# Adding the softmax constant on ScalarE, and a wider spacing of the second batch's attention steps

## The chip, the cores and the metric

One core of a Trainium2 chip runs the whole program. The metric is the device time of one execution in microseconds; three runs of the kernel before give the median. TensorE is called PE here, VectorE DVE, ScalarE ACT, GpSimd POOL and SyncE, which issues loads, SP.

## What is computed

Attention over chunks of 32 tokens with a little context and 8 memory slots, then a feed-forward layer, then a layer of eight experts in which every token goes to one expert. Cut to what matters:

```python
k_full = np.concatenate([mem_k, k_ctx], axis=2)
scores = scale * np.matmul(q_c, k_full.transpose(0, 1, 3, 2))
a = np.exp(scores - np.max(scores, axis=-1, keepdims=True))
a = a / (np.sum(a, axis=-1, keepdims=True) + 1e-09)
out[:, :, c_start:c_end] = np.matmul(a, v_full)
...
h = x @ w_in
x = (h * (1.0 / (1.0 + np.exp(-h)))) @ w_out
...
out[mask] = np.maximum(x[mask] @ w1[e], 0.0) @ w2[e]
```

## The kernel before

The 3072 tokens are cut into 8 batches of 384. Attention of one batch is done as four pairs of heads, so there are 32 pairs, numbered i = 0 to 31. Pairs 0 to 3 are worked in a prologue; pairs 4n+4 to 4n+7 are worked during batch n of the feed-forward layer. One pair goes through these steps:

- S, `att_s`: the PE makes the scores in two halves (L199); the DVE adds the mask and finds the extremes (L204); ACT takes the exponential and accumulates the sums (L210).
- N, `att_n`: the constant is added to the six sums (L219, DVE), the reciprocal taken (L220, DVE), and POOL multiplies the pair's scores by it (L221).
- T, `att_t`: the PE transposes one half (three transposes, L229), and ACT copies it out of the bank (L240); in the prologue the DVE copies for pairs 0 and 1 (L238).
- A, `att_av`: the product with the values on the PE (L255); behind it X, `att_x`: ACT rounds it to xh (L274) and the DVE takes the rest xl (L275), which the feed-forward layer needs.

The feed-forward layer of a batch runs in 16 steps g. `gemm1` (L297) makes a block of 128 hidden values for 384 tokens from xh and xl in bank h0 or h1; `swish` is a tanh on ACT (L306), a product on the DVE (L308), a rounding on ACT (L315) and the rest on POOL (L316); `gemm2` (L333) of step g - 2 adds to the output.

During the prologue and the first batch the weights are also prepared, in 32 items, two in each step. `tick` does four stages for four different items: `w_split` (ACT L161, POOL L162), `w_bits` (three DVE operations, L151, L152 and L154), `w_bias` (ACT L145) and `w_load` (SP). Every stage needs the one before, and the bias's bank is free again when the bits of an earlier item are done.

The schedule is manual: each engine runs its instructions in the order in which the program writes them. In the prologue that order is the string `PRO`, whose letters are the steps above, with w1 for a bias, w2 for bits and w3 for a split; the loops below it write the order of the batches. A step has three places: 0 ahead of the step's first tick and gemm1, 1 between gemm1 and the second tick, 2 behind gemm2. In the first batch the swish stands behind place 2. A pair's steps go to the places `3 * s0 + slot`, counted in thirds of a step; `PN`, `PT` and `PU` are the slots of N and of the two halves of T, and their first entries are for the first batch. There all scores, transposes and products of pairs 4 to 7 use the bank a0.

Of the kernel before, what the change touches and what calls it, by code (L numbers as in the profile page):

```python
# [7 lines left out]
F32 = mybir.dt.float32  # L8
# [4 lines left out]
AF = mybir.ActivationFunctionType  # L13
OP = mybir.AluOpType
# [6 lines left out]
NF = 16  # L21
# [13 lines left out]
GTH = 7.0  # L35
SPL = 3
PN = (4, 3, 4, 4)
PT = (7, 7, 8, 10)
PU = (8, 7, 8, 10)
PRO = 'q0 k0a p1 m0a p2 i0a v0 p3 S0 w0 N0 S1 w0 v1 S2 z0 N1 w1 T0 S3 w0 N2 w2 d2 v2 w1 T1 A0 w3 N3 X0 T2a A1 w2 w0 v3 w1 X1 g00 T3a w3 w0 A2 w2 w0 w1 X2 g01 w3 w0 A3 w2 w1 g10 g11 X3 w3'  # L40
EARLY = (0, 1, 1, 2, 2, 3, 4)
FILL = (2, 4, 4, 4)
# [5 lines left out]
def body(ctx, tc, qk_in, v_in, wcat1, wcat2, wgt, consts, masks, iconst, bconst, out):  # L48
    nc = tc.nc
    PE, V, A, G, S = nc.tensor, nc.vector, nc.scalar, nc.gpsimd, nc.sync  # L50
    ctx.enter_context(tc.manual_schedule())

    def pool(name, bufs, side, stack=ctx):
        return stack.enter_context(tc.tile_pool(name=name, bufs=bufs, side=side, reuse_waits="tile"))
# [11 lines left out]
    const = pool("const", 1, "left")  # L66
# [7 lines left out]
    Lg = const.tile([128, 24, 8], F32, name="Lg")  # L74
    Lp = const.tile([128, 3, 8], F32, name="Lp")
    junk = const.tile([128, 512], BF16, name="junk")
    wg_sum = const.tile([128, 512], F32, name="wg_sum")

    wg2 = const.tile([128, NF, 16], F32R, name="wg2")
# [136 lines left out]

    def att_n(i):
        s, m = pend.pop(i)
        V.tensor_scalar(out=m[:, 12:18], in0=m[:, 6:12], scalar1=1.0e-9, scalar2=None, op0=OP.add)  # L219
        V.reciprocal(out=m[:, 18:24], in_=m[:, 12:18])  # L220
        G.tensor_tensor(out=s, in0=s, in1=m[:, 18:24].unsqueeze(2).to_broadcast([128, 6, 96]), op=OP.mult)  # L221
        Sb[i] = s
# [274 lines left out]
    for op in PRO.split():  # L497
# [9 lines left out]
        elif c == "m":  # L507
            e.dma_start(msk, masks)
        elif c == "i":
            e.dma_start(ident, consts)  # L510
        elif c == "z":
            S.dma_start(x2d[0:1, :], zero[0:1, 0:1024].bitcast(F32))
        elif c == "S":
            att_s(i, (take(), take()), spare[i - 1] if i else None)
        elif c == "N":
            att_n(i)
        elif c == "T":
            att_t(i, (take(), take()), e is S)
        elif c == "A":
            att_av(i, take(("A", i)))  # L520
        elif c == "X":
            att_x(i)
            free.append(held.pop(("A", i)))
        elif c == "w":
            k = stage[i]
            advance(i, take(("w", k)) if i == 1 else None)
            if i == 2:
                free.append(held.pop(("w", k)))
        elif c == "g":
            if "h%d" % i in free:  # L530
                free.remove("h%d" % i)
            gemm1(0, i, (int(op[2]),))
        elif c == "d":
            b = bank(take())
            for _ in range(i):
                PE.matmul(b[:, 0:224], zero[:, 0:128], zero[:, 0:224], start=True, stop=True)
# [3 lines left out]
    for i in range(4, 4 * NB):  # L540
        n, hp = divmod(i - 4, 4)
        last = n == NB - 2
        s0 = NF * n - EARLY[n] + (SPL * hp if last else 11 * hp // 3 if n == 0 else 4 * hp)
        tight = last or i % 4 == 0 and EARLY[n] > EARLY[n - 1]
        kind = 0 if n == 0 else 1 if not last else 2 if hp < 3 else 3

        pa = 11 if n == 0 or last and hp < 3 or n < NB - 2 and hp == 3 and EARLY[n + 1] > EARLY[n] else 13
        av = "a0" if n == 0 or last and hp == 3 else "a2"

        tags = ("a0", "a1") if n else ("a0", "a0")  # L550
        scores = [(att_s, 1, tags, None, (0,)), (att_s, 2, tags, None, (1,))] if n == 0 else [(att_s, 2 if tight else 1)]
        for what, slot, *k in (*scores, (att_n, PN[kind]), (att_t, PT[kind], tags, False, (0,)),
                               (att_t, PU[kind], tags, False, (1,)), (att_av, pa, av)):
            part.setdefault(divmod(3 * s0 + slot, 3), []).append((what, i, *k))
    for g in range((NB - 1) * NF):
        n, f = divmod(g, NF)
        if g == NF:
            wg_open()
        last = n == NB - 2
# [12 lines left out]
        if g >= 2:  # L572
            m, k = divmod(g - 2, NF)
# [512 lines left out]
    n = NB - 1  # L1086
# [156 lines left out]
```

## Time and profile before

| what | value |
|---|---|
| median of 3 runs | 998.54 us (998.32 to 998.63) |
| profiled execution | 999.0 us, its span 997.2 us |
| mean granted clock of the PE | 0.989 |
| busy share | PE 97%, DVE 69%, POOL 42%, ACT 41% |
| chain that ended last | PE 82%, DVE 9%, issue 4%, ACT 3% |

The page cuts the span into 40 slices of 25 us. In the first four the PE is busy for 7 to 9 tenths and the DVE for 6 to 8; from the fifth on the PE is busy for 9 tenths or more almost throughout. Busy time alone doesn't tell who waits for whom: for that the timeline of an engine gives each instruction with its start, its length and, in brackets, the idle time before it with what ended it.

### The profile page before, as it was taken

What the parts mean: (1) busy time and instruction counts of PE and PEld (TensorE: products, weight loads), DVE (VectorE), ACT (ScalarE), POOL (GpSimd) and SP (SyncE); (2) the same over time, 40 slices, a digit from 0 to 9 for tenths busy, and PEclk for the clock granted to TensorE, in tenths of its full rate; (3) what the DMA queues carried; (4) which work ended last, traced back from release to release, by engine and by line L of the source; (5) the groups of instructions that cost most, each with busy time, mean ns of one, the idle gap of its engine ahead of it and who ended that gap; (6) DMA issues with size and microseconds to landing.
All of it is one profiled execution on the core that took longest, in us unless ns stands there. A gap on an engine that the chain in (4) does not pass through costs nothing.

```text
span 997.2 us, 19115 instructions
## 1 busy us (share of the span) xinstructions
PE 962.4 (97%) x7193; PEld 840.3 (84%) x7193; DVE 683.6 (69%) x1951; ACT 404.9 (41%) x1001; POOL 423.2 (42%) x335
## 2 busy tenths in 40 slices
PE   7799999999999999999999999998999999999997
PEld 5587788998898988888988987777788888999996
DVE  6888578988898988898248674676677787532110
ACT  7667543443444343444443431023333333443441
POOL 3566523232332333222223341144564664777771
PEclk8999999999999999999999999999999999999999
DMA  8667221111212111111121400316353444555420
GB/s 280 212 218 235 101 91 50 47 64 34 63 64 64 33 64 47 50 64 61 36 97 35 167 14 2 127 43 193 110 164 117 139 148 122 179 166 167 150 74 32
DMA packets 34062, 102.86 MB, mean 103 GB/s; under 512 B 4146, under 2 KB 7858, under 8 KB 33971
## 3 DMA queue, kind: packets, MB, share of 16 engines
q1 hardware_dynamic: 29698, 88.63, 28.0%
q0 software_dynamic: 3840, 12.59, 3.7%
q8 instruction: 56, 0.92, 0.4%
q10 hardware_dynamic: 432, 0.43, 0.2%
q14 instruction: 36, 0.29, 0.1%
HBM read 86.69 MB, written 14.94 MB: 102 GB/s over the span
## 4 chain that ended last, share of the span: by engine, by line
PE 82%; DVE 9%; issue 4%; ACT 3%; POOL 1%; DMA 0%; POOLq 0%; DVEq 0%
PE acc L333 23%; PE h L297 23%; PE h L1041 13%; PE acc L1068 12%; PE a L769 3%; PE a L255 2%; PE a L229 2%; PE a L199 2%; DVE a L152 2%; DVE a L151 2%; DVE w L154 1%; DVE junk L428 1%; ACT s L210 1%; PE a L966 1%; ACT spare L210 1%
## 5 line engine op out<-in xcount | busy, mean ns | idle before, releaser
L297 PE MATMUL h<-xh,big 128*128 128x384 f32 x1024 | 289.3, 343 | 2.7 <-DVE th L308 2.7
L316 POOL TENSOR_TENSOR gl<-th,gh 128x384 fp32r<-128x384 f32 x112 | 123.9, 1106 | 252.5 <-ACT gh L315 248.7
L333 PE MATMUL acc<-big,gh 128*128 128x512 f32 x636 | 201.9, 398 | 1.2 <-ACT w L398 1.2
L297 PEld LDWEIGHTS h<-xh,big 128*128 128x128 f32 x1024 | 189.7, 190 | 11.5 <-DVE th L308 4.8
L1014 POOL TENSOR_TENSOR big<-w,big 128x1024 fp32r<-128x1024 f32 x64 | 152.5, 2396 | 78.1 <-ACT big L1013 69.0
L297 PE MATMUL h<-xl,big 128*128 128x384 f32 x512 | 174.4, 341 | 0.0
L333 PEld LDWEIGHTS acc<-big,gh 128*128 128x128 f32 x636 | 115.3, 188 | 21.8 <-ACT w L398 1.6
L333 PE MATMUL acc<-big,gl 128*128 128x512 f32 x318 | 124.8, 392 | 0.0
L1068 PE MATMUL acc<-big,gh 128*128 128x512 f32 x384 | 123.8, 398 | 0.0
L1041 PE MATMUL h<-xh,big 128*128 128x384 f32 x512 | 117.7, 345 | 2.0 <-DVE gl L1050 1.3
L306 ACT ACTIVATE th<-h 128x384 f32<-128x384 f32 x128 | 62.4, 487 | 132.8 <-PE h L297 129.6
L308 DVE SCALAR_TENSOR_TENSOR th<-th,h 128x384 f32<-128x384 f32 x128 | 69.8, 546 | 66.3 <-ACT th L306 66.2
L428 DVE SCALAR_TENSOR_TENSOR junk<-wg_sum,w 128x512 bf16<-128x512 f32 x128 | 112.7, 881 | 3.3
L315 ACT ACTIVATE gh<-th 128x384 fp32r<-128x384 f32 x112 | 58.8, 525 | 126.7 <-DVE th L308 126.7
L297 PEld LDWEIGHTS h<-xl,big 128*128 128x128 f32 x512 | 97.3, 190 | 3.9 <-DVE xl L275 0.6
L1041 PEld LDWEIGHTS h<-xh,big 128*128 128x128 f32 x512 | 90.9, 189 | 6.9 <-DVE gl L1050 1.6
L1045 ACT ACTIVATE gh<-h 128x384 fp32r<-128x384 f32 x64 | 31.5, 492 | 153.9 <-PE h L1041 151.7
L1050 DVE SCALAR_TENSOR_TENSOR gl<-h,gh 128x384 fp32r<-128x384 f32 x64 | 35.3, 553 | 82.7 <-ACT gh L1045 82.3
L417 DVE SCALAR_TENSOR_TENSOR junk<-w 128x512 bf16<-128x512 f32 x96 | 85.4, 889 | 2.3
L1068 PEld LDWEIGHTS acc<-big,gh 128*128 128x128 f32 x384 | 70.6, 188 | 9.3
L1068 PE MATMUL acc<-big,gl 128*128 128x512 f32 x192 | 76.2, 397 | 0.0
L210 ACT ACTIVATE s<-s,m 128x96 f32<-128x96 f32 x168 | 60.8, 363 | 26.5 <-DVE m L204 26.5
(217 smaller groups left out, 1448.3 us busy)
## 6 DMA issues: line engine op xcount, KB each, us to landing
w<-in_wcat SPq DMA_DIRECT2D x96, 512.0 KB, 3.9
qk<-in_qk_in SPq DMA_DIRECT2D x28, 480.0 KB, 4.3
v<-in_v_in SPq DMA_DIRECT2D x28, 288.0 KB, 3.1
x2d<-w SPq DMA_DIRECT2D x16, 256.0 KB, 2.1
w<-in_wgt SPq DMA_DIRECT2D x4, 512.0 KB, 6.7
x2d<-x SPq DMA_DIRECT2D x8, 256.0 KB, 2.4
back<-gd SPq DMA_DIRECT2D x2, 768.0 KB, 5.3
big<-in_qk_in SPq DMA_DIRECT2D x3, 480.0 KB, 6.0
```

Of the source, the lines that this page charges most:

```text
L210: A.activation(out=s[:, b, :], in_=s[:, b, :], func=AF.Exp, scale=-1.0, bias=m[:, b:b + 1], accum_out=m[:, 6 + b:7 + b])
L297: PE.matmul(b[:, :TB], w1[:, o:o + 128], (xh, xl, xh)[p][:, c, :], start=not done, stop=len(done) == 11)
L306: A.activation(out=th, in_=b[:, :TB], func=AF.Tanh, scale=0.5)
L308: V.scalar_tensor_tensor(out=u, in0=th, scalar=1.0, in1=b[:, :TB], op0=OP.add, op1=OP.mult)
L315: A.activation(out=gh, in_=u, func=AF.Copy)
L316: G.tensor_tensor(out=gl, in0=u, in1=gh.bitcast(F32), op=OP.subtract)
L333: PE.matmul(a, g[:, 128 * t:128 * t + 128], w2[:, o:o + 512], start=(f in first and p == 0), stop=(f + 1 in (*first, NF) and p == 2))
L417: V.scalar_tensor_tensor(out=junk, in0=xs[k], scalar=1.0, in1=late["w"][e], op0=OP.mult, op1=OP.mult, accum_out=Lg[:, k, e:e + 1])
L428: V.scalar_tensor_tensor(out=junk, in0=t, scalar=0.5, in1=late["w"][e], op0=OP.mult, op1=OP.mult, accum_out=part2[:, f % 4, e:e + 1])
L1014: G.tensor_tensor(out=l, in0=t, in1=h.bitcast(F32), op=OP.subtract)
L1041: PE.matmul(b[:, :TB], (h, h, l)[p][:, 128 * c:128 * c + 128], (xh, xl, xh)[p][:, c, :], start=(p == 0 and c == 0), stop=(p == 2 and c == 3))
L1068: PE.matmul(a, (gh, gh, gl)[p][:, 128 * t:128 * t + 128], (h, l, h)[p][:, 512:1024], start=(s % 8 == 0 and p == 0), stop=(s % 8 == 7 and p ...
```

## The change

The constant 1e-9 is added to the softmax sums by ACT instead of the DVE, for all 32 pairs: an Identity activation whose bias is a new tile of one column. In the first batch (pairs 4 to 7) the pairs start at steps 0, 4, 8 and 12 instead of 0, 3, 7 and 11, and both halves of T move one place later, to slots 8 and 9. The last pair's product stands at slot 10 instead of 11, which is step 15, place 1 (before: step 14, place 2).

```diff
-PT = (7, 7, 8, 10)
-PU = (8, 7, 8, 10)
+PT = (8, 7, 8, 10)
+PU = (9, 7, 8, 10)
...
+    tiny = const.tile([128, 1], F32, name="tiny")
+    V.memset(tiny, 1.0e-9)
...
     def att_n(i):
         s, m = pend.pop(i)
-        V.tensor_scalar(out=m[:, 12:18], in0=m[:, 6:12], scalar1=1.0e-9, scalar2=None, op0=OP.add)
+        A.activation(out=m[:, 12:18], in_=m[:, 6:12], func=AF.Identity, bias=tiny)
         V.reciprocal(out=m[:, 18:24], in_=m[:, 12:18])
...
-        s0 = NF * n - EARLY[n] + (SPL * hp if last else 11 * hp // 3 if n == 0 else 4 * hp)
+        s0 = NF * n - EARLY[n] + (SPL * hp if last else 4 * hp)
...
+        if n == 0 and hp == 3:
+            pa = 10
```

## Rows read from the trace of the kernel before

**Rows 1.** The chain that ended last, 0 to 120 us: shares by engine and line.

```profile
by line: DVE a L152 13.0%; DVE a L151 12.5%; issue 10.5%; DVE w L154 9.4%; ACT s L210 6.8%; PE h L297 5.6%; ACT spare L210 5.5%; PE acc L333 3.8%; ACT big L161 3.4%; DMA big<-in_qk_in 3.2%; ACT a L145 3.1%; DVE th L308 2.9%; DVE m L219 2.8%
```

**Rows 2.** Stretches: length, busy us of PE, PEld, DVE, ACT, POOL; granted clock, DMA share, GB/s.

```profile
120.00:220.00 100.00, 100.00 (x718) 89.54 (x716) 83.81 (x238) 41.55 (x124) 31.69 (x28) 1.00 0.23 78
```

**Rows 3.** Timeline of the DVE, prologue: start us, length us, line, operation, operands, idle before.

```profile
11.50 0.17 DVE L219 TENSOR_SCALAR junk<-junk 128x6 f32<-128x6 f32 x1 [0.37 <-ACT spare L210]
...
11.82 0.97 DVE L238 COPY big<-a 96x384 f32<-96x384 f32 x2
...
13.11 0.26 DVE L204 CUSTOM_DVE_ANT_0 spare<-acc,msk 128x96 f32<-128x96 f32 x1 [0.32 <-PE acc L199]
...
14.49 0.67 DVE L151 TENSOR_SCALAR a<-a 128x512 int32<-128x512 int32 x1
...
17.65 0.19 DVE L220 RECIPROCAL junk<-junk 128x6 f32<-128x6 f32 x1
```

**Rows 4.** Timeline of ACT, prologue.

```profile
13.44 0.19 ACT L210 ACTIVATION_READ_ACCUMULATOR spare<-spare,junk 128x1 f32 x1
...
14.09 0.36 ACT L210 ACTIVATE spare<-spare,junk 128x96 f32<-128x96 f32 x1
...
16.15 0.19 ACT L210 ACTIVATION_READ_ACCUMULATOR spare<-spare,junk 128x1 f32 x1
```

**Rows 5.** Timeline of POOL, prologue and step 4.

```profile
17.54 1.30 POOL L162 TENSOR_TENSOR big<-w,big 128x512 fp32r<-128x512 f32 x1 [1.67 <-ACT big L161]
...
54.81 1.32 POOL L162 TENSOR_TENSOR big<-w,big 128x512 fp32r<-128x512 f32 x1
```

**Rows 6.** Timeline of the DVE, first batch: swishes (L308) and one tensor_scalar.

```profile
33.30 0.55 DVE L308 SCALAR_TENSOR_TENSOR th<-th,h 128x384 f32<-128x384 f32 x1 [1.27 <-ACT th L306]
...
52.64 0.56 DVE L308 SCALAR_TENSOR_TENSOR th<-th,h 128x384 f32<-128x384 f32 x1 [1.27 <-ACT th L306]
...
55.24 0.93 DVE L219 TENSOR_SCALAR m<-m 128x6 f32<-128x6 f32 x1
...
58.42 0.55 DVE L308 SCALAR_TENSOR_TENSOR th<-th,h 128x384 f32<-128x384 f32 x1
...
63.15 0.55 DVE L308 SCALAR_TENSOR_TENSOR th<-th,h 128x384 f32<-128x384 f32 x1
...
68.36 0.55 DVE L308 SCALAR_TENSOR_TENSOR th<-th,h 128x384 f32<-128x384 f32 x1
...
75.51 0.56 DVE L308 SCALAR_TENSOR_TENSOR th<-th,h 128x384 f32<-128x384 f32 x1 [1.27 <-ACT th L306]
...
113.39 0.54 DVE L308 SCALAR_TENSOR_TENSOR th<-th,h 128x384 f32<-128x384 f32 x1
```

**Rows 7.** Timeline of ACT, steps 4 and 5.

```profile
55.36 0.66 ACT L161 ACTIVATE big<-w 128x512 fp32r<-128x512 f32 x1 [0.51 <-DVE w L154]
...
62.28 0.46 ACT L240 ACTIVATE at<-a 96x384 f32<-96x384 f32 x1
```

**Rows 8.** Timeline of the PE, steps 3 and 13 to 15.

```profile
49.99 0.71 PE L199 MATMUL a<-qk 64*64 64x96 f32 x12 [1.88 <-DVE xl L275]
...
106.78 0.53 PE L229 MATMUL a<-ident,s 128*96 128x128 f32 x3 [0.80 <-ACT at L240]
...
111.42 0.92 PE L255 MATMUL a<-at,v 96*64 96x64 f32 x24
...
116.64 0.73 PE L199 MATMUL a<-qk 64*64 64x96 f32 x24
```

**Rows 9.** Stretches around idle times of the PE, columns as in Rows 2.

```profile
48.10:50.00 1.90, 0.03 (x4) 0.01 (x2) 1.49 (x3) 1.24 (x3) 1.30 (x1) 1.00 0.84 196
...
50.00:54.20 4.20, 4.20 (x24) 4.08 (x25) 2.15 (x9) 2.53 (x9) 0.37 (x1) 0.61 0.87 284
...
78.90:84.20 5.30, 2.92 (x16) 2.16 (x16) 4.99 (x10) 3.13 (x8) 4.25 (x5) 1.00 0.55 175
```

**Rows 10.** Groups by line on ACT, whole run: xcount, busy us, mean ns, idle before.

```profile
L210 ACT ACT_TABLE_LOAD x1 | 1.3, 1283 | 2.2 <-issue 2.2
```

## The prediction

> **What bounds the kernel now.** I read the chain of waits first, for the first 120 us. There DVE and ACT lines stand: the three bit operations on the weights (L151, L152, L154), the exponentials (L210), the casts [rows 1]. From the second transposes of the last head pair (106.78) on, the chain holds nearly only matmul lines, and in the hundred microseconds from 120 the PE is busy without a break [rows 2]. So what the change does before the scores of pair 8 (116.64, [rows 8]) moves the end by as much; what it adds to later batches lies beside a PE that never waits. I then read the DVE row by row. I mark step g of the first batch by the start of its swish on the DVE, th(g): th(0) at 33.30 [rows 6].
>
> **The addend in the prologue.** ACT and DVE run strictly in the order of the program. In the written order the sums of pair 1 are finished (N1) behind the scores and exponentials of pair 2 (S2). On the DVE that cost nothing: the tensor_scalar at 11.50 waited only for pair 1's own sums, 0.37 us [rows 3]. On ACT the add of pair 1 now queues behind six exponentials of pair 2, whose last accumulator read ends at 13.44 + 0.19 = 13.63 [rows 4], and the DVE's reciprocal, with all that is behind it, waits for it.
>
> No row has such an add. Its length is that of an accumulator read at the least, 0.19, and of an exponential with a pointer bias at the most, 0.36 [rows 4]; I take 0.28, halfway, as it has the form of the one and the length of the other. The sum: pair 0's add takes the place of a 0.17 tensor_scalar [rows 3], so all is 0.11 late; 13.63 + 0.11 + 0.28 + 0.07 (an estimate for two hand-overs) = 14.09 for the reciprocal of pair 1. Behind it on the DVE stand 0.11 of that reciprocal, the two copies of T0 (0.97, 0.04 of it overlapped) and the reductions of S3: 15.13 instead of 13.11 [rows 3]. S3's exponentials follow by one reduction, 0.26: 15.39 instead of 14.09; they take 16.15 + 0.19 - 14.09 = 2.25 [rows 4], to 17.64. Pair 2's add is behind them: 17.64 + 0.28 + 0.07 + 0.11 = 18.10 for the first bit operation, which before began at 14.49 [rows 3]. That is 3.6 late; with 0.19 for an add 3.3, with 0.36 3.9. I take 3.5, since a tenth can vanish where ACT's first split stood ready behind other work. From there to th(0) DVE, ACT and POOL hand the chain to each other with little idle time, and the loads are far ahead, so th(0) comes at 36.8.
>
> **The addend in the loop.** Here it pays. The tensor_scalar of pair 5 takes 0.93 [rows 6], though its twin in the prologue takes 0.17; it ends at 56.17, where the POOL's subtraction ends (54.81 + 1.32, [rows 5]). The other three of this loop are like it. The reciprocal doesn't inherit that: one ran 0.19 at 17.65 [rows 3] with the POOL busy from 17.54 to 18.84 [rows 5]. The add finds ACT idle, 0.51 before the split at 55.36 [rows 7], so it is hidden there; without that cover it would cost 0.28. So a step with N, which took 58.42 - 52.64 = 5.78 [rows 6], loses the 0.93 and the hand-over of 0.03 behind it: 4.82.
>
> **Four steps apart.** Pair 5's scores used to share step 3 with pair 4's product, in one bank, and the PE waited 1.88 for it [rows 8]. Now every pair has its own step for scores (75.51 - 68.36 = 7.15 from swish to swish), for N (4.82), a plain one (63.15 - 58.42 = 4.73) and one for the product and its split (68.36 - 63.15 = 5.21) [rows 6]. By the DVE alone th(12) would be 65.7 behind th(0).
>
> **The transposes one place later.** Both halves use bank a0, so the second half waits until ACT has copied the first out. Before, that copy stood between two pairs of split and bias, and a whole gemm2 covered the wait on the PE. Now the first half is the last PE work of its step and the second the first of the next: nothing lies between. And the copy stands behind the second split, which waits for the DVE's bits. Its new place in ACT's queue is that of the second copy of before, 62.28, 3.86 behind the swish at 58.42 [rows 6, 7]; with 0.46 for the copy the second half starts 4.4 behind that swish, u. Behind it on the PE stand gemm1, gemm2 and then the product: 111.42 - 106.78 = 4.64 [rows 8]. From the product's start to the swish behind its split are 113.39 - 111.42 = 1.97 [rows 6, 8]. So th comes at u + 11.0 where the DVE alone would reach it at u + 4.73 + 5.21 = u + 9.94: 1.07 lost per pair, three times. SP's loads are issued earlier or later with their steps and have many microseconds.
>
> **The sum.** Three pairs, 3 x (4.82 + 11.0) + 2 x 7.15 = 61.8 from th(0) to th(11). The product of pair 6 starts 1.97 ahead of th(11); from there the PE has product, gemm1 and gemm2 (116.64 - 111.42 = 5.22, [rows 8]), two more pairs of gemm1 and gemm2 (4.64 less 0.3 for the transposes, 4.35 each) and two score halves of 0.65, 15.2 in all (0.3 and 0.65 are estimates, the 0.53 and 0.73 of [rows 8] less what matmuls overlap): pair 7's first half at th(11) + 13.25. ACT copies it behind a rounding and the last split (0.66, [rows 7]), by estimate at th(13) + 1.7 = th(11) + 13.65, so the second half starts at 14.2; from there to the scores of pair 8 are 116.64 - 106.78 - 4.35 = 5.5 [rows 8]. That makes 61.8 + 19.7 = 81.5 for what took 116.64 - 33.30 = 83.3: 1.8 won against 3.5 lost in the prologue, +1.7.
>
> **The clock.** Pair 5's and 6's first half comes 13.25 behind the swish of the product step and takes 0.3, the second 7.15 + 4.82 + 4.4 = 16.4 behind it: the PE idles 2.8; for pair 4, whose first half follows a gemm1 that waited for th(0), some 2.2. After 1.90 idle (48.1 to 50.0) the granted clock was 0.61 over 4.2 us, partly at 1.2 GHz; the stretch from 78.9 to 84.2, with 5.30 - 2.92 = 2.4 idle in two pieces, stayed at 1.00, 2.4 GHz [rows 9]. The new gaps are longer than the one that lowered it, and what runs behind them (gemm1, gemm2, product) is just what the DVE then waits for. A fall costs up to 4.2 x 0.39 = 1.6; I take 1.5 for each, 4.5 for three. In all +1.7 + 4.5 = +6.2 on the profiled execution's 999.0, or 1005.2. That execution (span 997.2, the rest around it) is 0.5 above the median of the runs, so the forecast is 1004.7.
>
> **Rivals.** (a) The clock falls after one or two of the gaps only: 1001.7 or 1003.2. For it: the two shorter pieces at 78.9 did nothing. (b) It falls after none: 1000.2. Against it stands the 1.90 of [rows 9]. The Trainium skill, in "TensorE: Matmul & The Clock Gate", section "HAM oscillation", has a rule of thumb on which idle gaps let the clock fall; at its word none of these three would, and the time would be that of (b). The trace speaks against the rule. (c) Not slower: the transposes' wait is covered and the DVE alone sets the pace. It decides at u + 3.3: with the second half there by then, product and split are in time, 3 x 1.07 = 3.2 and the 4.5 are not paid: +1.7 - 3.2 = -1.5, 997.0. Only ACT's written order speaks against it. (d) As (c), and the prologue's reciprocals don't wait for the other pair's exponentials, so three adds (0.84) are all that is lost: 0.84 - 1.8 - 3.2 = -4.2, 994.3. (e) The new function needs a table of its own: the one load in the whole run took 1.28 [rows 10], two for each of 32 pairs would be 82. Copies, Relu, Exp and Tanh run behind that single load, which speaks against it. The Trainium skill ("ScalarE: Activation LUTs", section "Table sets: the hidden batching unit") says that cheap functions, identity among them, are in every set, so this stays at 0.03; no run here has shown it for this function.
>
> **How the numbers follow.** Forecast 0.40, (a) 0.25, (b) 0.15, (c) 0.12, (d) 0.05, (e) 0.03. What a measurement of this kernel tells from no change is about 0.2%, 2 us. Forecast, (a) and (e) are slower by more, 0.68; (b) and (c) are within it, 0.27; (d) is faster, 0.05. The range leaves out (c), (d) and (e), 0.20 together: it goes from (b) with a second and a bit less of stall, 999.0, to the forecast with the dearer add and the full 1.6, 1006.5.
>
> **What would show it.** Right: reciprocals of pairs 1 and 2 near 14.1 and 18.0, th(0) near 36.8; N steps of 4.8; the second transposes waiting over 2 us for ACT's copy, the DVE then waiting for ACT's xh; the granted clock near 0.6 behind them; scores of pair 8 near 118 without falls and 122.8 with three. Wrong: a th(0) under 34, second transposes under 1 us of wait, a clock of 1.00 throughout, or more than one table load.

## The result, and the profile after

The changed kernel takes 1003.85 us (median of 6 runs, 1002.9 to 1005.09) against 998.6 of the kernel before; the ratio is 1.0051, interval 1.0039 to 1.0064. It is slower by 5.2 us; the forecast was 1004.7, in a range from 999.0 to 1006.5. The profiled execution, 1005.09 with a span of 1003.3, is the longest of the six, 1.2 above the median, so its trace can show more loss than a usual run has. Line numbers of kernel.py are 2 higher than before (the swish's product is L310, the second transposes' wait is at L231, ACT's copy at L242).

The prologue, on the DVE (start, length, what; in brackets the idle time ahead and what ended it):

```profile
13.82 0.19 DVE L222 RECIPROCAL junk<-junk 128x6 f32<-128x6 f32 x1 [2.71 <-ACT junk L221]
17.59 0.19 DVE L222 RECIPROCAL junk<-junk 128x6 f32<-128x6 f32 x1 [1.63 <-ACT junk L221]
17.70 0.68 DVE L153 TENSOR_SCALAR a<-a 128x512 int32<-128x512 int32 x1
```

and on ACT:

```profile
13.50 0.28 ACT L221 ACTIVATE junk<-junk,tiny 128x6 f32<-128x6 f32 x1
...
17.27 0.28 ACT L221 ACTIVATE junk<-junk,tiny 128x6 f32<-128x6 f32 x1
```

The reciprocals of pairs 1 and 2 stand on the DVE with 2.71 and 1.63 us of idle time ahead of them, and what ends it each time is ACT's add (L221), which starts only when ACT is through with the six exponentials of the next pair. The first bit operation starts at 17.70; before it was 14.49 [rows 3].

The loop, on the DVE:

```profile
36.52 0.56 DVE L310 SCALAR_TENSOR_TENSOR th<-th,h 128x384 f32<-128x384 f32 x1 [1.27 <-ACT th L308]
...
41.33 0.55 DVE L310 SCALAR_TENSOR_TENSOR th<-th,h 128x384 f32<-128x384 f32 x1
...
53.39 0.56 DVE L277 TENSOR_TENSOR xl<-a,xh 128x384 fp32r<-128x384 f32 x1 [2.47 <-ACT xh L276]
...
53.87 0.54 DVE L310 SCALAR_TENSOR_TENSOR th<-th,h 128x384 f32<-128x384 f32 x1
...
61.01 0.55 DVE L310 SCALAR_TENSOR_TENSOR th<-th,h 128x384 f32<-128x384 f32 x1 [1.27 <-ACT th L308]
...
63.61 0.18 DVE L222 RECIPROCAL m<-m 128x6 f32<-128x6 f32 x1
...
65.83 0.55 DVE L310 SCALAR_TENSOR_TENSOR th<-th,h 128x384 f32<-128x384 f32 x1
...
78.33 0.54 DVE L310 SCALAR_TENSOR_TENSOR th<-th,h 128x384 f32<-128x384 f32 x1
```

The rows of before to set beside these are [rows 6]: th(0) comes at 36.52 instead of 33.30. A step with N takes 65.83 - 61.01 = 4.82; in it stands only a reciprocal of 0.18. A step with scores takes 61.01 - 53.87 = 7.14. From the swish of the N step to that of the product step it is 53.87 - 41.33 = 12.54, then 12.50, where the DVE alone would need 9.94: at 53.39 it stood idle for 2.47 us until ACT had xh.

Why xh is late is seen on the PE:

```profile
45.69 0.53 PE L231 MATMUL a<-ident,s 128*96 128x128 f32 x3 [3.79 <-ACT at L242]
...
70.19 0.88 PE L231 MATMUL a<-ident,s 128*96 128x128 f32 x3 [2.68 <-ACT at L242]
...
94.65 0.88 PE L231 MATMUL a<-ident,s 128*96 128x128 f32 x3 [2.66 <-ACT at L242]
...
122.42 0.72 PE L201 MATMUL a<-qk 64*64 64x96 f32 x24
```

and in the stretches around the first two of these waits (length, busy us of PE, PEld, DVE, ACT, POOL, then the granted clock):

```profile
41.90:45.70 3.80, 0.01 (x2) 0.01 (x1) 3.52 (x6) 3.25 (x7) 3.65 (x4) 1.00 0.69 230
45.70:51.00 5.30, 5.30 (x21) 5.07 (x22) 4.95 (x8) 3.66 (x7) 3.99 (x4) 0.68 0.70 209
67.50:70.20 2.70, 0.02 (x2) 0.02 (x1) 2.46 (x5) 2.17 (x5) 2.69 (x3) 1.00 0.59 199
70.20:75.00 4.80, 4.80 (x19) 4.65 (x20) 4.52 (x8) 3.54 (x7) 3.65 (x4) 0.65 0.69 217
```

The second halves of the transposes wait 3.79, 2.68 and 2.66 us for ACT's copy (L242) of the first; before, the longest such wait was 0.80 [rows 8]. The clock is 1.00 (2.4 GHz) in these two gaps and falls behind them to a mean of 0.68 and 0.65, so part of the time is at 1.2 GHz, just where gemm1 and gemm2 run, behind which the late product stands. The scores of pair 8 start at 122.42, before at 116.64 [rows 8]: 5.8 us of the span's 6.1 are lost by then.

### The profile page after: what moved, and what is told of

Read it like the earlier page. It is cut to its first block, busy times and chain, and to the rows that moved or that the text cites. A ratio compares the mean times of both kernels' runs of the same rounds, so it can differ in the third digit from the quotient of the medians.

```text
span 1003.3 us, 19093 instructions
## 1 busy us (share of the span) xinstructions
PE 964.2 (96%) x7193; PEld 840.3 (84%) x7193; DVE 675.2 (67%) x1920; ACT 413.3 (41%) x1033; POOL 423.8 (42%) x335
## 4 chain that ended last, share of the span: by engine, by line
PE 82%; DVE 10%; issue 3%; ACT 3%; POOL 1%; POOLq 0%; DVEq 0%; ACTq 0%
PE acc L335 23%; PE h L299 23%; PE h L1045 12%; PE acc L1072 12%; PE a L773 3%; PE a L257 2%; DVE junk L419 2%; PE a L231 2%; PE a L201 2%; DVE junk L430 1%; DVE a L154 1%; DVE a L153 1%; PE a L970 1%; ACT s L212 1%; DVE w L156 1%
## 5 line engine op out<-in xcount | busy, mean ns | idle before, releaser
L308 ACT ACTIVATE th<-h 128x384 f32<-128x384 f32 x128 | 62.3, 487 | 132.5 <-PE h L299 122.8
L310 DVE SCALAR_TENSOR_TENSOR th<-th,h 128x384 f32<-128x384 f32 x128 | 69.9, 546 | 68.8 <-ACT th L308 68.5
```

The lines of the kernel that those rows point to most:

```text
L308: A.activation(out=th, in_=b[:, :TB], func=AF.Tanh, scale=0.5)
L310: V.scalar_tensor_tensor(out=u, in0=th, scalar=1.0, in1=b[:, :TB], op0=OP.add, op1=OP.mult)
```

## The experiments

Runs of one group were made on one chip beside the kernel before. Its median was 998.9 for the first four, 1006.4 for the next three and 1004.9 for the last four (the chips differ), so the ratio to before is what can be compared throughout. It is the ratio on record, with its interval, and not always the exact quotient of the two medians beside it (for e7 that would be 1.0157).

| run | what it is | us | before, same chip | ratio (95%) |
|---|---|---|---|---|
| the change | | 1003.85 | 998.6 | 1.0051 (1.0039 to 1.0064) |
| e1_prologue | before + add on ACT, pairs 0 to 3 | 1001.25 | 998.9 | 1.0023 (1.0013 to 1.0034) |
| e2_loop | before + add on ACT, pairs 4 to 31 | 995.01 | 998.9 | 0.9963 (0.9948 to 0.9977) |
| e3_schedule | change, add on the DVE | 1004.16 | 998.9 | 1.0058 (1.0041 to 1.0075) |
| e4_old_T | change, T at its old slots | 997.11 | 998.9 | 0.9980 (0.9970 to 0.9989) |
| e5_best | e4, add on the DVE for pairs 0 to 3 | 1002.52 | 1006.4 | 0.9960 (0.9943 to 0.9976) |
| e6_add_early | change, add behind its own exponentials | 1012.63 | 1006.4 | 1.0052 (1.0032 to 1.0073) |
| e7_busy | change + matmuls that nobody reads, behind ACT's copy | 1022.22 | 1006.4 | 1.0140 (1.0114 to 1.0166) |
| e8_busy_ahead | change + matmuls that nobody reads, ahead of the copy | 1006.15 | 1004.9 | 1.0015 (1.0005 to 1.0025) |
| e9_early_pro | e6 for pairs 0 to 3 alone | 1007.56 | 1004.9 | 1.0026 (1.0014 to 1.0038) |
| e10_best_again | e5_best once more | 1001.09 | 1004.9 | 0.9960 (0.9945 to 0.9975) |
| e11_loop_again | e2_loop once more | 1001.29 | 1004.9 | 0.9966 (0.9953 to 0.9979) |

**The add, in the prologue alone and in the loop alone.** Both are the kernel before with one half of the first edit (the tile `tiny` is made as in the change); e1 is shown, e2 has `if i >= 4` in its place:

```diff
-        V.tensor_scalar(out=m[:, 12:18], in0=m[:, 6:12], scalar1=1.0e-9, scalar2=None, op0=OP.add)
+        if i < 4:
+            A.activation(out=m[:, 12:18], in_=m[:, 6:12], func=AF.Identity, bias=tiny)
+        else:
+            V.tensor_scalar(out=m[:, 12:18], in0=m[:, 6:12], scalar1=1.0e-9, scalar2=None, op0=OP.add)
```

> The kernel before with one part of the change: the constant is added by ACT for pairs 0 to 3 only. Theory (the reciprocals wait behind the next pair's exponentials, 3.2 us by th(0) 33.30 before and 36.52 after): th(0) near 36.5, scores of pair 8 near 119.9, time 998.6 + 3.2 = 1001.8. Rival (the loop takes the delay up in its idle time): th(0) late, but scores of pair 8 near 116.6 and a time within 999.0. Second rival (the wait is hidden in the prologue): th(0) under 34.

> The kernel before with ACT adding the constant for pairs 4 to 31 only. Theory (each of four N steps loses 0.96 us of the DVE, and the DVE sets the pace up to the last pair's transposes): steps with N take 4.82 instead of 5.78, scores of pair 8 3.8 earlier, near 112.8, time 994.8. Rival (the PE's own waits at transposes and at the shared bank are the bound of the loop): the swishes come no more than 1 us earlier, time 997.6 or more.

Measured: 1001.25 and 995.01, ratios 1.0023 and 0.9963. The scores of pair 8, on the PE of e1, then of e2:

```profile
119.95 0.73 PE L201 MATMUL a<-qk 64*64 64x96 f32 x24
```

```profile
112.00 0.73 PE L201 MATMUL a<-qk 64*64 64x96 f32 x24
```

3.3 later and 4.6 earlier than 116.64. In e2's loop the DVE has the 0.18 reciprocal where a 0.93 tensor_scalar stood [rows 6]:

```profile
50.72 0.56 DVE L313 SCALAR_TENSOR_TENSOR th<-th,h 128x384 f32<-128x384 f32 x1 [1.27 <-ACT th L311]
...
53.32 0.18 DVE L225 RECIPROCAL m<-m 128x6 f32<-128x6 f32 x1
...
55.53 0.55 DVE L313 SCALAR_TENSOR_TENSOR th<-th,h 128x384 f32<-128x384 f32 x1
```

55.53 - 50.72 = 4.81 for the step. So the first edit holds a loss of 2.3 us in the prologue and a gain of 3.7 us in the loop, and neither rival stands: the loop doesn't take up the prologue's delay, and the DVE, not the PE, sets the loop's pace.

**The schedule alone, and the change with the old slots of T.**

```diff
 e3_schedule, from the changed kernel
-        A.activation(out=m[:, 12:18], in_=m[:, 6:12], func=AF.Identity, bias=tiny)
+        V.tensor_scalar(out=m[:, 12:18], in0=m[:, 6:12], scalar1=1.0e-9, scalar2=None, op0=OP.add)
 e4_old_T, from the changed kernel
-PT = (8, 7, 8, 10)
-PU = (9, 7, 8, 10)
+PT = (7, 7, 8, 10)
+PU = (8, 7, 8, 10)
```

> The changed kernel with the constant added by the DVE as before: only the spacing of four steps, the later transposes and the last product's place are left of the change. Theory (the second transposes wait for ACT's copy, and the clock falls behind the gap): N steps 5.78, three steps with a product about 7.5 where the DVE alone takes 5.2, scores of pair 8 at 121.7 to 123.5, time 1003.5 to 1005.1. Rival (the addend is the cost of the change, the schedule alone a gain by the parted product and scores): time 997.4, 1.2 below before.

> The changed kernel with both halves of T back at slots 7 and 8; spacing of four, addend on ACT and the last product's place as changed. Theory (the place of the transposes is what costs in the loop): second transposes wait under 1 us, granted clock 1.00 from 40 to 110 us, steps with a product 5.2, th(0) still at 36.5; 3.2 lost in the prologue against 5.1 won in the loop: time 996.7. Rival (the spacing or the addend costs, the transposes' place does nothing): 1003 to 1004.

Measured: 1004.16 and 997.11, and both times are as the theory had them. The traces agree in part. In e3's, the shortest of its four runs, the scores of pair 8 start at 121.01, ahead of the 121.7 expected, since the clock stayed at 1.00 behind the third gap (last section). In e4's, the longest of its ten, they start at 116.68, because one product step took 6.94 instead of 5.21. Who waited for whom from 30 to 118 us (total us, times, longest), in the change, e3 and e4:

```profile
PE a L231 <- ACT at L242: 9.7, 4, 3.8
```

```profile
PE a L231 <- ACT at L242: 11.8, 4, 3.6
```

```profile
PE a L231 <- ACT at L242: 0.5, 3, 0.2
```

With T at the new slots the PE waits 9.7 and 11.8 us for ACT's copies, with T at the old ones 0.5, and between the change and e4, which differ in T alone, the ratio moves by 0.0071, some 7 us. The spacing is not what costs. Added up by ratio, +2.3 for the add in the prologue, -3.7 for it in the loop and +5.8 for the schedule make +4.4 where the change measures +5.1; the intervals are wide enough for the difference.

In the long product step of e4's trace something new ended a wait, on ACT:

```profile
73.34 0.62 ACT L147 ACTIVATE a<-w 128x512 f32<-128x512 f32 x1 [1.99 <-DMA w<-in_wcat]
```

The bias waited 1.99 us for a load of weights. Neither kernel, before nor after, waits for such a load between 33 and 112 us.

**The parts that won, together.** e5 is e4 with `if i >= 4` for the add on ACT, as in e2.

> The parts that won, together: ACT adds the constant for pairs 4 to 31, the DVE for pairs 0 to 3; spacing of four; both halves of T at slots 7 and 8 as before; the last product's place as changed. Theory (the prologue's delay and the transposes' place are the two losses, the N steps and the parted scores and product the two gains): th(0) near 33.3, scores of pair 8 5.1 earlier than before, near 111.5, time 998.8 - 5.1 = 993.7, below the 995.0 of the loop's addend alone. Rival (without the DVE's stalls the PE becomes the bound and takes the spacing's 1.2 back): 995.0.

> The same kernel as e5_best, beside e2_loop on one chip. Theory (the spacing is worth another 0.5 to 1.3 us over the loop's addend alone, scores of pair 8 at 111.5 against 112.0 in the traces): ratio to before 0.9950, under that of e2_again. Rival (no difference that can be measured): the two intervals lie within each other, 0.996.

> The same kernel as e2_loop, as the comparison for e10_best_again: ratio to before 0.996, scores of pair 8 at 112.0.

Measured: ratio 0.9960 in both tries, 0.9966 for the loop's addend alone beside it; the intervals lie over each other, so e5 beats both kernels, but whether the spacing adds anything to e2 can't be told. In e5's first trace the scores of pair 8 start at 111.50, as expected, in the second at 112.42 against 112.02 of e11. From th(0) to these scores are 78.9 and 79.9 us in e5's two traces, against 79.7 in e2's and in e11's. In the traces the loads take the spacing's gain back, and not the PE as the rival had it: two product steps of the second trace took 6.29 and 5.56 instead of 5.21, one of the first 5.63, and without these excesses both would be at 78.5. In the second trace ACT waited for weights twice, 1.9 us, once like this:

```profile
68.69 0.63 ACT L147 ACTIVATE a<-w 128x512 f32<-128x512 f32 x1 [1.33 <-DMA w<-in_wcat]
```

**The place of the add in ACT's queue.**

```diff
 e6_add_early, from the changed kernel: in att_s, behind the exponentials
         if halves[-1] == 1:
+            A.activation(out=m[:, 12:18], in_=m[:, 6:12], func=AF.Identity, bias=tiny)
             del qk[i]
 in att_n
-        A.activation(out=m[:, 12:18], in_=m[:, 6:12], func=AF.Identity, bias=tiny)
```

e9 does the first only `if i < 4` and leaves the add in `att_n` for the others.

> The changed kernel with the add moved within ACT's queue: it stands behind the exponentials of its own pair, not where N is written; reciprocal and all else stay. Theory (the prologue loses by the add's place in the queue behind the next pair's exponentials, not by its length): reciprocals of pairs 1 and 2 near 11.8 and 14.5, th(0) near 33.9, some 0.2 more in each of the steps with scores (the add is ahead of the tanh), time 1003.85 - 2.6 + 0.6 = 1001.8. Rival (ACT is simply full in the prologue, every add and its waits cost wherever they stand): th(0) stays at 36, 1003.9.

> The changed kernel with the add behind the exponentials of its own pair for pairs 0 to 3 only; in the loop it stays where N is written, so it isn't ahead of the tanh as in the run before. Theory (the prologue's loss is the add's place in the queue): th(0) near 34.1, steps with scores 7.15, time 2.4 below the changed kernel, ratio to before 1.0027. Rival (what the prologue gives back is lost again in the loop): ratio 1.005.

Measured: e6 1.0052, no gain; e9 1.0026, in size the gain expected. In e6 the prologue does what was expected, reciprocals at 11.80 and 14.28 and th(0) at 34.09:

```profile
11.80 0.19 DVE L222 RECIPROCAL junk<-junk 128x6 f32<-128x6 f32 x1 [0.70 <-ACT junk L215]
14.28 0.19 DVE L222 RECIPROCAL junk<-junk 128x6 f32<-128x6 f32 x1
...
34.09 0.56 DVE L310 SCALAR_TENSOR_TENSOR th<-th,h 128x384 f32<-128x384 f32 x1 [1.60 <-ACT th L308]
```

but in the loop the add now stands ahead of the tanh for which the DVE waits: 1.60 at 34.09 where it was 1.27 [rows 6], and as much in each step with scores; and in the traced run the second product came later still (77.22 - 63.61 = 13.6 instead of 12.5), with a granted clock of 0.50 from 68 to 73 us. So the time is the rival's, but not for its reason. e9 avoids the first loss. Its trace, though, confirms the mechanism only up to the reciprocals (12.04 and 14.52): th(0) is at 36.14, because here the PE ran at half its clock in the prologue's last part and the DVE had to wait for it:

```profile
31.58 0.26 DVE L206 CUSTOM_DVE_ANT_0 s<-a,msk 128x96 f32<-128x96 f32 x1 [1.47 <-PE a L201]
...
36.14 0.55 DVE L313 SCALAR_TENSOR_TENSOR th<-th,h 128x384 f32<-128x384 f32 x1 [1.27 <-ACT th L311]
```

This is the stretch in e9, and then the same of e6:

```profile
22.00:31.00 9.00, 9.00 (x71) 7.70 (x71) 7.24 (x12) 5.32 (x10) 3.90 (x3) 0.52 0.60 182
```

```profile
22.00:31.00 9.00, 6.82 (x88) 5.37 (x82) 8.60 (x19) 6.07 (x17) 3.92 (x3) 0.91 0.70 226
```

Nor is e9's gain, in its trace, the one expected. The scores of pair 8 start 2.05 earlier than in the changed kernel (120.37), but only 0.38 of that is there at th(0); 1.6 come from the first product step, 51.90 - 40.95 = 10.95 instead of 12.54, since pair 4's gap was 2.25 us here and the clock stayed at 1.00 behind it. So the queue's place is shown to be the cause of the late reciprocals, and e1 that they cost time; that the early add wins this back at the end is not shown.

**The clock by itself.** Idle matmuls (products of the unit matrix with itself into columns that nothing reads) between the halves leave the wait as it is and keep the PE at work. In e7 they stand behind ACT's copy in the program, in e8 ahead of it:

```diff
 e8_busy_ahead, from the changed kernel: in att_t, ahead of the copy
+            if h == 0 and 4 <= i < 7:
+                for _ in range((13, 8, 8)[i - 4]):
+                    PE.matmul(b[:, 384:512], ident, ident, start=True, stop=True)
             if dve:
```

> The changed kernel with idle work for the PE between the halves of T: 14, 10 and 10 products of the unit matrix with itself, behind the first half of pairs 4, 5 and 6, into columns of bank a0 that nothing reads. The wait for ACT's copy stays. Theory (of the 1.07 and 1.5 us per pair the 1.5 is the clock's): granted clock 1.00 behind the second halves, a step with product 6.3 instead of 7.8, so 4.5 less: 999.4. Rival (the clock's fall is beside the path, the wait alone costs): the time stays at 1003.9. Second rival (the added products hold the second halves back): over 1003.9.

> The changed kernel with idle work for the PE between the halves of T, now ahead of ACT's copy in the program, so that it need not wait for the copy as in the run before: 13, 8 and 8 products of the unit matrix with itself, about 0.21 us each, into columns of bank a0 that nothing reads. The wait for the copy stays. Theory (1.5 us per pair is the clock's): granted clock 1.00 behind the second halves, 10.97 from the swish of the N step to that of the product step instead of 12.5, time 4.5 below the changed kernel, ratio to before 1.0006. Rival (the clock's fall is beside the path, the wait alone costs): ratio stays at 1.005.

e7 doesn't answer the question, as its second rival came true: the products waited for the copy out of the same bank, as the second halves do, and ran behind the gap instead of in it:

```profile
45.44 5.02 PE L246 MATMUL a<-ident 128*128 128x128 f32 x28 [3.78 <-ACT at L242]
50.52 0.53 PE L231 MATMUL a<-ident,s 128*96 128x128 f32 x3
```

They put 5.1 us in front of pair 4's second half and some 4.1 in front of the next two, and the time went up by some 9 us over the changed kernel (1.0140 against 1.0051): what stands there is on the path. In e8 they fill the gap but for its last 0.9 us:

```profile
41.54 3.07 PE L241 MATMUL a<-ident 128*128 128x128 f32 x26
45.51 0.53 PE L231 MATMUL a<-ident,s 128*96 128x128 f32 x3 [0.90 <-ACT at L245]
```

The second half still starts at its old place behind the swish (45.51 - 41.13 = 4.38; in the changed kernel 45.69 - 41.33 = 4.36), so the wait is as it was. The clock isn't:

```profile
45.60:51.00 5.40, 5.40 (x48) 4.68 (x48) 4.83 (x8) 3.54 (x7) 3.90 (x4) 1.00 0.74 209
```

and on the DVE the product step's swish follows 52.13 - 41.13 = 11.0 behind the N step's instead of 12.5:

```profile
41.13 0.55 DVE L313 SCALAR_TENSOR_TENSOR th<-th,h 128x384 f32<-128x384 f32 x1
...
52.13 0.55 DVE L313 SCALAR_TENSOR_TENSOR th<-th,h 128x384 f32<-128x384 f32 x1
```

Ratio 1.0015 instead of 1.0051: 3.6 us, and 4.5 us in the place of pair 8's scores (117.92 against 122.42). The new slots of T lose 7.1 us by ratio against e4, and 5.7 in the place of these scores (122.42 against 116.68). So the fall of the clock is half of that loss by ratio, and more in the traces.

## Why the prediction was right, point by point

- **The bound.** The scores of pair 8 moved by +5.8, the span by +6.1; in e1 and e2 the shift there is +3.3 and -4.6, the time's +2.3 and -3.7. From these scores to the end of the span are 880.6 us before, 880.9 in the change, 879.8 in e1 and 880.4 in e2, so what is lost or won up to that point stays, within 1 us for a single run.
- **The add's length.** Taken as 0.28 between 0.19 and 0.36; measured 0.28 to 0.30 in all 32 places, and no second table load in the run.
- **The prologue.** Forecast reciprocals at 14.1 and 18.0, th(0) 3.5 late; measured 13.82, 17.59 and 3.2. Two terms were a little too large: pair 1's add starts 0.09 behind the start of the last accumulator read (13.41), not behind its end, and the 0.11 for pair 0's add doesn't show, as that read starts no later than before (13.44). From the first bit operation on, the DVE's own work carries the delay, as forecast: its idle time up to th(0) is 2.0 us, before 1.9, although the PE ran at half clock beside it. The 3.2 is a difference of two single traces: from pair 0's reciprocal to th(0) are 24.5 us in the trace of before, 24.0 to 24.2 in e2, e3, e5, e10 and e11, whose prologue is the same, and 27.5 to 27.7 with the adds on ACT (the change, e1, e4, e7, e8). In time the prologue's adds cost 2.3 us (e1, interval 1.3 to 3.4).
- **N in the loop.** 4.82 forecast, 4.82 measured. The reciprocal at 63.61 ran 0.18 while the POOL subtracted, so it didn't inherit the 0.93:

```profile
63.18 1.32 POOL L164 TENSOR_TENSOR big<-w,big 128x512 fp32r<-128x512 f32 x1
```

  The Trainium skill ("SBUF — State Buffer", section "SBUF: two separate sides") says that the DVE in a two-port mode and the POOL hold a shared port in turn, each for a whole instruction; the tensor_scalar of before, which ended with the POOL's subtraction [rows 5, 6], agrees, though no trace here shows in which mode it ran.
- **The transposes.** The second half 4.4 behind the swish: measured 4.36. The product step's swish at u + 11.0 with a full clock: 11.0 in e8. The stall of 1.07 and its cause are right: by ratio e8 lies 3.5 us above e4, where T stands as before, and 3 x 1.07 = 3.2 were forecast.
- **The gaps.** 2.8 forecast for pairs 5 and 6, 2.68 and 2.66 measured. For pair 4 I put 2.2; it was 3.79, since I had let the gemm1 ahead of it run at half clock as in the kernel before, and it ran at full.
- **The clock.** 1.5 for each of three falls; in the traced run the product steps took 1.5, 1.5 and 1.3 more than in e8's 11.0. Over runs it is less: the median lies 1.2 below the traced run and the six spread over 2.2 us. The six lie on both sides of rival (a)'s 1003.2, the median between it and 1004.7 and a little nearer to (a). The one trace has three falls; how many the untraced runs had isn't known, so the times alone don't decide between the forecast and (a) with two falls. That the median came within 0.9 us of the forecast is in part luck.
- **The sum.** Loop from th(0) to the scores of pair 8: forecast 81.5 + 4.5 = 86.0, measured 122.42 - 36.52 = 85.9; before 83.3.
- **The loads.** They were taken to have many microseconds. In the change nothing waited for them between 33 and 112 us; in e4, e5, e6, e8, e9 and e10 ACT did, by 0.2 to 2.0 us, so the room was smaller than thought.
- **The range.** Its upper end, 1006.5, is not what its terms give: the dearer add (0.4) and 0.1 more for each of three falls make 1005.4. The measured 1003.85 lies within either.
- **The rivals.** (b) is what e8 makes: +1.5 by ratio, forecast +1.7. (c), the DVE's pace alone, is e4, where T stands as before: forecast -1.5, measured -2.0. (d), both losses gone, is e5: forecast -4.2 with three adds left, measured -4.0 with none; in its traces the loads take back a part. (e) didn't occur.

## What to carry to other kernels

Moving a short operation to another engine moves it into that engine's queue: before counting what it frees, look for what stands ahead of it there and who waits behind it on both engines; here the same edit won 3.7 us where ACT was idle and lost 2.3 us where it queued behind other exponentials. Two steps that share one bank need other work written between them on the engine that waits, and the copy that frees the bank needs a place in its queue that doesn't hang on something later. A gap in matmuls can cost more behind it than in it, when what follows at half the clock is what the others wait for; filling the gap with idle matmuls measures that part by itself.

## What the runs showed of the hardware that was not expected

- The length of a gap doesn't settle whether the clock falls. After 2.7 idle us in the changed kernel it was 0.65; in e3 the last of three gaps, 3.6 of 4.5 us idle, was followed by 1.00:

```profile
90.00:94.50 4.50, 0.86 (x7) 0.81 (x7) 4.22 (x7) 3.47 (x7) 3.57 (x3) 1.00 0.53 151
94.50:99.00 4.50, 4.50 (x42) 3.83 (x42) 4.12 (x7) 3.18 (x6) 3.60 (x3) 1.00 0.71 215
```

  In e9 it was 1.00 behind a gap of 2.25, while before a gap of 1.90 was followed by 0.61 [rows 9]. What decides wasn't tried. Whether it is what makes such kernels scatter from run to run (2.2 us here, 3.6 in e3) isn't shown either: e4, without such gaps, scatters by 3.0.
- Weight loads, which nothing waited for in either kernel between 33 and 112 us, made ACT wait 2.0, 1.1, 0.9 and 1.9 us in that stretch of e4, e5, e8 and e10, and 0.2 and 0.5 in e6 and e9. All six have the spacing of four, and those with the quickest loop wait most: the first four steps took 21.9 us in e4, e5 and e10, 23.0 and 22.9 in e8 and e9, 24.7 in e6. The change and e3, with the same spacing and 24.5 and 25.4 us, show no such wait, nor do e1, e2 and e11 with the old spacing. SP itself waits for the POOL's subtraction (L164), which frees the buffer of a load, 50.0 us in all in e4 and 46.1 in e11; whether that is what holds the loads back wasn't tried.
- The prologue's last part runs at half clock in some runs: the granted clock from 16 to 26 us was 0.51 in the changed kernel and 0.83 before. From 22 to 31 us it was 0.52 in e9 and 0.91 in e6, and e9's th(0) is 2 us later than e6's.
